# The second pair of layer one in block products of two units, with its weight parts in DRAM and the next layer's x operands made from chunks in DRAM

## The chip, the core and the metric

The program runs on one core of a Trainium2 chip. The metric is the device time of one execution in microseconds (us); of several runs the median is given. A profiled execution gives the trace, and its span runs from the first instruction to the last.

## The reference

Sigmoid attention, then two feed-forward layers on 1792 tokens (4 sequences of 448) of 768 channels, 2048 hidden units each. Everything is float32.

```python
scores = scale * q @ k.T - log(S)          # 4 x 12 heads, S = 448, D = 64
x = (1 / (1 + exp(-scores))) @ v           # heads side by side: 1792 x 768
h = x @ w1_in;  x = relu(h) ** 2 @ w1_out
h = x @ w2_in;  out = (max(h, 0) + alpha * min(h, 0)) @ w2_out
```

The weights come in as 64-bit words, whose halves the kernel joins to float32 itself (`raw` to `words`: two ScalarE scalings, one VectorE join).

## The kernel before

Every float32 product is made of three TensorE products of rounded parts, high x high, high x low and low x high (`HIGH + LOW`), so each operand is first split: ScalarE copies the high part, VectorE or GpSimd subtracts to get the low one.

The feed-forward work is cut into 32 units. A unit is (layer, pair, fp): a pair is two sequences (896 tokens), fp is one of 8 groups of 256 hidden units (two `j` of 128). This gives four stages of eight units, called here 1A and 1B (layer one, first and second pair) and 2A and 2B (layer two). A unit has an inward part (x by w_in) and an outward part (hidden by w_out, added to the output `acc`).

**Inward** (`add_inward`, `product`): the product of 256 hidden units by 896 tokens over 768 channels is done as 2 x 2 blocks with seven block products in place of eight. `X[0..6]` hold the parts of seven x operands (three 128-channel chunks each), `W` those of seven weight operands (`OPERAND` slots). Each of the seven products is nine matmuls of 448 columns into a bank `h`. `x_sum` and `x_high`/`x_low` make the x operands from the pair's `acc`; for the next stage some of them are made ahead by GpSimd (`add_waiting`) through `stage` and kept in DRAM (`kept_x`). `weight_sum`, `weight_high` and `weight_low` make the weight operands of a unit from `words`.

**Outward**, two forms. In stages 1A, 1B and 2A (`add_outward`, `out_product`) a unit's hidden block `G[j]` meets `WO[j]` at once: per j three ways, in layer one with 512 or 384 tokens as moving columns, twelve outputs. In 2B only, `out_block` treats two neighbouring units together: their hidden values are left unsplit in `E[0]` and `E[1]`, sums of blocks are made, and seven block products of 18 matmuls each replace eight. Parts of hidden sums go through a ring of `G` slots, parts of weight sums through a ring of `WO` slots; `collect` and `gather` add the banks to `acc`. Its weight operands come from DRAM: 2A stores `W` (`kept_w`) and 2B loads it (`add_weights_kept`); layer two's words are loaded and joined during 1B (`add_words`) and recalled in 2A (`add_recall`).

The order of all this is set by `Plan`: each step is a job with an engine, an estimated duration, what it reads and writes. `Plan.run` gives each job a due time counted back from TensorE's own fixed order, and fills every engine's queue by due time; SP's queue issues the DMAs in that order, and each engine works its queue in order.

Of the kernel before, what the change touches and what calls it, by code (L numbers as in the profile page):

```python
# [19 lines left out]
class Plan:  # L20
# [4 lines left out]

    HOP = 0.10
    MARGIN = 3.0
# [19 lines left out]
    def run(self):  # L47
# [6 lines left out]
        def length(j):  # L54
            return jobs[j][1] if jobs[j][0] != "SP" else jobs[j][5] / 0.28e6 + 2.0
# [24 lines left out]
        def choose(e):  # L80
# [8 lines left out]
            for j in now:  # L89
                end = t + jobs[j][1]  # L90
                if not any(due[s] < due[j] and begin(s, free[e]) < end and end > due[s] - self.MARGIN for s in soon):
                    return t, j
# [3 lines left out]
        while len(order) < n:  # L96
            t, j, e = min((*c, e) for e in engines if (c := choose(e)))
# [8 lines left out]
            if e == "SP" or size:  # L106
                dma_free = max(dma_free, t + 0.1) + size / 0.28e6
                end = dma_free + 2.0
# [12 lines left out]
def fused_kernel(ctx: ExitStack, tc: tile.TileContext, q, k, v, w1i, w1o, w2i, w2o, alpha, out):  # L121
# [47 lines left out]
    W = wpool.tile([P, 2, 7 * HALF], F32R, name="wi")  # L169
    sums = wpool.tile([P, 4 * HALF], F32, tag="sums", name="sums")  # L170
    both_words = wpool.tile([P, 4 * DM], F32, name="words")
    words = {kind: both_words[:, i * 2 * DM:(i + 1) * 2 * DM].rearrange("p (j m) -> p j m", j=2) for i, kind in enumerate("io")}
    raw = [wpool.tile([P, DM, 2], I32, tag=f"raw{i}", name=f"raw{i}") for i in range(2)]
    late = dpool.tile([P, NC * PAIR], F32, name="late")
    kept = {}
# [3 lines left out]
    def load(at, n, kind, j):  # L179
# [4 lines left out]
        d = raw[at].rearrange("p m t -> p (m t)").bitcast(I64)  # L184
# [5 lines left out]
    def scale(at, word):  # L190

        half = raw[at][:, :, word]
        if word:
            nc.scalar.activation(half.bitcast(F32), half.bitcast(F32), AF.Prelu, scale=2.0 ** -112, alpha=2.0 ** 32)  # L194
        else:
            nc.scalar.activation(half, half.bitcast(U32), AF.Copy, scale=2.0 ** -29 * (1 - 2.0 ** -12), bias=-0.5 + 7.5 * 2.0 ** -12)  # L196

    def joined(at, n, kind, j):

        if UNITS[n][0] == 0:  # L200
            return words[kind][:, j].bitcast(I32)
        return raw[at].rearrange("p m t -> p (m t)")[:, :DM]

    def join(at, n, kind, j):

        nc.vector.scalar_tensor_tensor(out=joined(at, n, kind, j), in0=raw[at][:, :, 1], scalar=3, in1=raw[at][:, :, 0], op0=ALU.logical_shift_left, op1=ALU.bitwise_or)
# [66 lines left out]
    with tc.manual_schedule():  # L273
# [6 lines left out]
        with tc.tile_pool(name="apool", bufs=1) as apool, tc.tile_pool(name="apsum", bufs=1, space=bass.MemoryType.PSUM) as psum:  # L280
# [153 lines left out]
            for d in range(ND):  # L434
# [37 lines left out]
                if item:  # L472
                    join(i % 2, *item)
                    keep(i % 2, *item)
# [38 lines left out]
        def product(k, bank, halves):  # L513

            ps = hb[bank][:, :S]
            for c in range(KH):
                at = OPERAND[k] * HALF + c * P
                for i, (wp, xp) in enumerate(((0, 0), (0, 1), (1, 0))):
                    ends = [0, S // 2, S] if halves and c == 0 and i == 0 else [0, S]
                    for a, e in zip(ends, ends[1:]):  # L520
                        nc.tensor.matmul(ps[:, a:e], W[:, wp, at:at + P], X[k][:, xp, c, a:e], start=(k in OPENING and c == 0 and i == 0 and a == 0), stop=(c == KH - 1 and i == 2), skip_group_check=True)  # L521
# [55 lines left out]
        LAST = NU - NB  # L577

        def blocks(n):

            return (UNITS[n][2] % 2, False) if n >= LAST else (0, True)

# [11 lines left out]

        def cells_of(p, name, c):
            kh, t = PLACE[name]
            return [("acc", p, ((kh * KH + c) * 2 + t) * S // CELL + k) for k in range(S // CELL)]
# [15 lines left out]
        def add_words(n, kind, j):  # L613

            at = at_raw[0] % 2
            at_raw[0] += 1
            high, low = ("raw", at, 1), ("raw", at, 0)
            layer, p, fp = UNITS[n]
            to = [("words", kind, j)] if layer == 0 else [high, low]
            add("SP", 0.05, lambda: load(at, n, kind, j), [], [high, low], size=2 * DM * BYTES)  # L620
            add("ACT", act(DM), lambda: scale(at, 1), [high], [high])
            add("ACT", act(DM), lambda: scale(at, 0), [low], [low])
            add("DVE", dve(DM), lambda: join(at, n, kind, j), [high, low], to, port=True)
            add("SP", 0.05, lambda: keep(at, n, kind, j), to, [("kept", layer, 2 * fp + j, kind)], size=DM * BYTES)

        def add_recall(n, kind, j):
            layer, p, fp = UNITS[n]
            add("SP", 0.05, lambda: recall(n, kind, j), [("kept", layer, 2 * fp + j, kind)], [("words", kind, j)], size=DM * BYTES)
# [3 lines left out]
        def add_weights(n):  # L632

            for what, reads in (("s12", ["s0", "s1"]), ("s34", ["s2", "s3"]), ("a1", [("words", "i", 0)]), ("a2", [("words", "i", 1)])):
# [5 lines left out]
                if UNITS[n][:2] == (1, 0):  # L640
                    a, e = SLOTS[what][0] * HALF, (SLOTS[what][-1] + 1) * HALF
                    to = w_kept[UNITS[n][2]] = w_kept.get(UNITS[n][2]) or dpool.tile([P, 2, 7 * HALF], F32, name=f"kept_w{n}")
                    add("SP", 0.05, lambda a=a, e=e, to=to: nc.sync.dma_start(out=to[:, :, a:e], in_=W[:, :, a:e].bitcast(F32)), [("w", s, i) for s in SLOTS[what] for i in range(2)], [("kept_w", UNITS[n][2], s) for s in SLOTS[what]], size=2 * (e - a) * BYTES)

# [14 lines left out]
        def add_weights_kept(n):  # L659

            for k in OPERAND:
# [377 lines left out]
```

## Time and profile before

| what | value |
|---|---|
| median of 3 runs | 1028.1 us (1028.08 to 1028.81) |
| the profiled execution's own time | 1027.84 us |
| its span | 1026.0 us |
| TensorE busy | 1019.7 us (99%) |
| VectorE, ScalarE, GpSimd busy | 710.3, 635.9, 297.4 us |
| DMA | 209.79 MB, mean 204 GB/s |
| TensorE clock granted | 1.0 throughout |

In the trace attention runs to 158.49 us; the four stages begin at 158.49, 377.73, 596.02 and 816.14 us (the first inward product of each). PE is TensorE, PEld its weight loads, DVE VectorE, ACT ScalarE, POOL GpSimd, SP the queue that issues the DMAs.

### The profile page before, as it was taken

To read this page: it belongs to the slowest core of one execution; us is meant where nothing else is said; L and a number is where in the kernel's file an instruction comes from. 1 tells how busy PE (TensorE), PEld (TensorE's weight loads), DVE (VectorE), ACT (ScalarE), POOL (GpSimd) and SP (SyncE) were. 2 spreads that over 40 slices of the span, in tenths; PEclk is the share of its full clock that TensorE was granted. 3 is DMA by queue.
4 is the path that set the end of the run, shared out by engine and by line. 5 is a ranking of instruction groups with operands and counts; after the bars stand their busy time and mean duration, and the time that the engine had idled before them with its cause. 6 is when DMAs were issued, how large, how long until landed. Compare 5 with 4: busy or idle time off the path is not lost.

```text
span 1026.0 us, 15038 instructions
## 1 busy us (share of the span) xinstructions
PE 1019.7 (99%) x5591; PEld 895.3 (87%) x5591; DVE 710.3 (69%) x951; ACT 635.9 (62%) x995; POOL 297.4 (29%) x258
## 2 busy tenths in 40 slices
PE   9999999999999999999999999999999999999998
PEld 5555558998999999999999999999999999999998
DVE  5555986567776775877666665777766667685857
ACT  4567778866776668666666767555545465535352
POOL 0001233364211142542111231354112207170603
PEclk9999999999999999999999999999999999999999
DMA  7577746566665785566555877688655882727133
GB/s 151 141 190 197 204 133 233 193 211 216 190 229 164 260 321 200 187 225 222 197 188 200 329 288 261 229 292 301 224 207 188 309 265 95 213 67 211 35 104 108
DMA packets 146584, 209.79 MB, mean 204 GB/s; under 512 B 56528, under 2 KB 115408, under 8 KB 144976
## 3 DMA queue, kind: packets, MB, share of 16 engines
q1 hardware_dynamic: 143632, 207.00, 61.3%
q10 hardware_dynamic: 2880, 1.84, 0.6%
q8 instruction: 44, 0.72, 0.3%
q14 instruction: 28, 0.23, 0.1%
HBM read 138.22 MB, written 70.58 MB: 204 GB/s over the span
## 4 chain that ended last, share of the span: by engine, by line
PE 88%; issue 3%; DMA 3%; DVE 3%; POOL 2%; ACT 1%; SPq 0%; POOLq 0%; DVEq 0%; ACTq 0%
PE h L521 35%; PE o L544 27%; PE o L863 6%; PE av L374 5%; PE sc L354 4%; PE h L863 4%; PE h L544 2%; POOL wo L649 1%; PE tp L321 1%; PE av L382 1%; PE scr L364 1%; DMA raw<-in_moe_w_out_dram 1%; PE tp L324 1%; DMA words<-kept21o 1%; DVE acc L785 1%
## 5 line engine op out<-in xcount | busy, mean ns | idle before, releaser
L521 PE MATMUL h<-x,wi 128*128 128x448 f32 (+1 forms) x2072 | 418.1, 360 | 0.1
L521 PEld LDWEIGHTS h<-x,wi 128*128 128x128 f32 x2072 | 380.0, 188 | 29.6 <-issue 0.7
L544 PE MATMUL o<-g,wo 128*128 128x512 f32 (+1 forms) x1056 | 223.3, 366 | 0.1
L544 PEld LDWEIGHTS o<-g,wo 128*128 128x128 f32 x1056 | 192.7, 188 | 23.2 <-DVE acc L785 0.5
L649 POOL TENSOR_TENSOR wo<-words,wo 128x384 fp32r<-128x384 f32 x96 | 99.4, 1066 | 236.5 <-ACT wo L652 235.1
L785 DVE TENSOR_TENSOR acc<-o,acc 128x768 f32<-128x768 f32 (+2 forms) x133 | 128.8, 973 | 24.2 <-PE o L544 23.7
L711 DVE TENSOR_TENSOR c<-h,c 128x448 f32<-128x448 f32 x84 | 52.3, 623 | 127.8 <-PE h L521 127.6
L544 PE MATMUL o<-wo,g 128*128 128x384 f32 x624 | 113.0, 335 | 0.4 <-DVE g L694 0.3
L544 PEld LDWEIGHTS o<-wo,g 128*128 128x128 f32 x624 | 109.1, 188 | 1.4 <-DVE g L694 1.0
L694 DVE TENSOR_TENSOR g<-c,g 128x448 fp32r<-128x448 f32 x96 | 64.3, 675 | 40.2 <-ACT c L682 34.2
L356 ACT ACTIVATE a<-sc,bias 128x896 f32<-128x896 f32 x72 | 69.2, 1005 | 35.6 <-PE av L374 22.6
L652 ACT ACTIVATE wo<-words 128x768 fp32r<-128x768 f32 x48 | 38.3, 840 | 84.2 <-PE o L544 52.9
L268 POOL TENSOR_TENSOR stage<-acc,stage 128x448 fp32r<-128x448 f32 x33 | 42.7, 1294 | 154.6 <-ACT stage L265 154.6
L707 ACT ACTIVATE c<-h 128x448 f32<-128x448 f32 x84 | 45.5, 543 | 55.4 <-PE h L521 55.1
L194 ACT ACTIVATE raw<-raw 128x768 f32<-128x768 f32 x64 | 57.8, 903 | 28.9 <-DMA raw<-in_moe_w_in_dram 20.0
L374 PE MATMUL av<-a,v 128*64 128x448 f32 x288 | 59.4, 548 | 0.0
L847 POOL TENSOR_TENSOR wo<-acc,wo 128x384 fp32r<-128x384 f32 x24 | 29.2, 1239 | 99.1 <-ACT wo L842 99.0
L196 ACT ACTIVATE raw<-raw 128x768 int32<-128x768 uint32 x64 | 57.5, 898 | 0.0
L261 POOL TENSOR_TENSOR acc<-acc 128x448 f32<-128x448 f32 x40 | 55.1, 1382 | 8.3 <-DMA acc<-late 6.3
L244 DVE TENSOR_TENSOR wi<-sums,wi 128x768 fp32r<-128x768 f32 x48 | 50.0, 1046 | 5.2 <-ACT wi L240 5.2
L690 DVE SCALAR_TENSOR_TENSOR c<-c,nal,pos 128x448 f32<-128x448 f32 x48 | 34.8, 726 | 14.9 <-ACT c L689 13.4
L268 POOL TENSOR_TENSOR x<-acc,x 128x448 fp32r<-128x448 f32 x15 | 18.1, 1218 | 88.3 <-ACT x L265 88.3
(140 smaller groups left out, 1393.6 us busy)
## 6 DMA issues: line engine op xcount, KB each, us to landing
raw<-in_moe_w_in_dram SPq DMA_DIRECT2D x32, 768.0 KB, 5.4
raw<-in_moe_w_out_dram SPq DMA_DIRECT2D x32, 768.0 KB, 5.6
wi<-kept_w SPq DMA_DIRECT2D x56, 384.0 KB, 4.2
kept_w<-wi SPq DMA_DIRECT2D x24, 768.0 KB, 5.3
kept_x<-stage SPq DMA_DIRECT2D x33, 448.0 KB, 4.2
x<-kept_x SPq DMA_DIRECT2D x11, 1344.0 KB, 10.3
v<-in_v_dram SPq DMA_DIRECT2D x24, 192.0 KB, 2.9
nat<-in_q_dram SPq DMA_DIRECT2D x22, 192.0 KB, 3.6
```

What stands on the lines that cost most here:

```text
L194: nc.scalar.activation(half.bitcast(F32), half.bitcast(F32), AF.Prelu, scale=2.0 ** -112, alpha=2.0 ** 32)
L196: nc.scalar.activation(half, half.bitcast(U32), AF.Copy, scale=2.0 ** -29 * (1 - 2.0 ** -12), bias=-0.5 + 7.5 * 2.0 ** -12)
L261: eng.tensor_sub(to, x, y)
L268: eng.tensor_sub(lo, x_block(p, X_FROM[i], c), hi)
L356: nc.scalar.activation(sig[u, j], ps[:, :, :S], AF.Sigmoid, bias=bias[:, :1], scale=SCALE)
L374: nc.tensor.matmul(avs[u][h * D:(h + 1) * D, :S], vals[u][:, h, j, :], a[:, h, :], start=(u % 2 == 0 and j == 0), stop=(u % 2 == 1 and j = ...
L521: nc.tensor.matmul(ps[:, a:e], W[:, wp, at:at + P], X[k][:, xp, c, a:e], start=(k in OPENING and c == 0 and i == 0 and a == 0), stop=(c == ...
L544: nc.tensor.matmul(ps, *ops, start=(begin and i == 0), stop=(end and i == len(ways) - 1), skip_group_check=True)
L649: nc.gpsimd.tensor_sub(WO[j][:, 1, at], words["o"][:, j, at], WO[j][:, 0, at])
L694: add("DVE", dve(S), lambda: nc.vector.tensor_sub(gl, e, gh), [*key, h_key], [l_key], port=True)
L785: add("DVE", dve(count), lambda dst=dst, src=src: nc.vector.tensor_add(dst, src, dst), [*src_keys, *cells], cells)
L863: nc.tensor.matmul(ps, left(gi, j), right(wi)[:, j], start=(start and j == 0 and i == 0), stop=(j == 1 and i == 2), skip_group_check=True)
```

## The change

1B takes the form of 2B. Its outward products go through `out_block`, in layer one with weight parts as the stationary operand and hidden parts as the moving one, 448 columns wide. `E[1]` and two weight sums (`TT`) lie in pair 0's `acc[0]` in both layers, so 1A's last unit stores `acc[0]` to DRAM (`hidden`), and 2A's x operands are made in 1B from chunks loaded back into a spare stretch of it (`pieces`): all seven for chunks 0 and 1, three for chunk 2, kept in DRAM. 1A stores its weight parts, 1B loads them. Layer two's words are in the main loaded, scaled and joined in 2A itself, the two inward ones by one transfer (`load_both`). X steps ahead of 2B are on VectorE in place of GpSimd (`X_BY`). The planner's transfer time follows the run length (`moved`), and its rules for SP and GpSimd change.

```diff
-    MARGIN = 3.0
+    MARGIN = 2.5
+    DEPTH = 3.0
 ...
+            if jobs[j][0] == "SP":
+                t = max(t, dma_free - self.DEPTH)
 ...
+                if e == "POOL" and give_way and any(jobs[s][4] and due[s] < min(due[j], end) and max(free["DVE"], ready[s]) < end for s in waiting["DVE"]):
+                    continue
 ...
+    def in_place(n, kind, j):
+        return UNITS[n][0] == 0 or UNITS[n][2] > 0 and (kind == "i" or j == 1)
 ...
+    PIECES = 4 * S + 2 * DM
+    pieces = acc[0][:, PIECES:PIECES + 4 * S].rearrange("p (k t s) -> p k t s", k=2, t=2)
 ...
+        def moved(size, run):
+
+            return size / run * (0.037 + run / 30e3) / 16
 ...
+                if fp == NB - 1 and layer == 0:
+                    c, at = os[0][0], TOKENS[os[0][1]]
+                    add("SP", 0.05, lambda part=part, c=c, at=at: nc.sync.dma_start(out=hidden.rearrange("p (c s) -> p c s", c=NC)[:, c:c + 2, at], in_=part), cells, [("hidden", cell[2]) for cell in cells], size=moved(2 * size * BYTES, 4 * size))
 ...
+            WIDE = MAIN if layer else S
+            RING = {"g": 2 + layer, "wo": 3 + layer}
 ...
-                    add("PE", 6 * PE_OUT[HALF], lambda i=i, left=left: matmuls(banks[at][i][:, :HALF], left, ws, start), gk + wk, [bank_keys[at][i]])
+                    def stationary(ways, j, i=i):
+                        return (gs(ways[0]) if layer else ws(ways[1]))[:, j, i * P:(i + 1) * P]
+
+                    def moving(ways, j):
+                        return (ws(ways[1]) if layer else gs(ways[0]))[:, j]
 ...
+        X_BY = ("POOL", "POOL", "DVE")
 ...
+            elif p:
                 add_weights_kept(n)
 ...
-            if NB <= n < 2 * NB:
-                for kind in "io":
-                    for j in range(2):
-                        add_words(n + NB, kind, j)
+            elif layer == 0:
+                for kind, j in (("i", 0), ("i", 1), ("o", 0), ("o", 1)) if fp == 0 else (("o", 0),):
+                    add_words(n + NB, kind, j)
 ...
-            outward = add_outward(n) if n < LAST else None
+            outward = add_outward(n) if p == 0 else None
 ...
-                    if i < (3 if layer else 4):
+                    chunks = KH if i < (3 if layer or by_pieces else 4) else KH - 1 if by_pieces else 0
```

How the order moves, first on TensorE (PE) after the last inward product of 1B's first unit before, and of its first two units now (`h`, `o`: banks; `g`: hidden parts; `wo`, `ring_sums`: slots of weight parts). Before:

```order
L521 MATMUL h_1790<-x_74,wi 128x448 x8
L544 MATMUL o_1789<-g_1786,wo_1784 128x384 x6
L544 MATMUL o_1793<-g_1786,wo_1784 128x384 x6
L544 MATMUL o_1794<-g_1786,wo_1784 128x384 x3
L544 MATMUL o_1794<-g_1785,wo_1783 128x384 x3
L544 MATMUL h_1792<-g_1786,wo_1784 128x384 x3
L544 MATMUL h_1792<-g_1785,wo_1783 128x384 x3
L544 MATMUL o_1789<-g_1786,wo_1784 128x512 x3
L544 MATMUL o_1789<-g_1785,wo_1783 128x512 x3
```

Now:

```order
L555 MATMUL h_1784<-x_74,wi 128x448 x9
L942 MATMUL o_1785<-g_1777,wo_1775 128x224 x2
L942 MATMUL o_1785<-g_1777,wo_1775 128x448 x11
L942 MATMUL o_1786<-g_1777,wo_1775 128x448 x6
L942 MATMUL h_1782<-g_1778,wo_1776 128x224 x2
L942 MATMUL h_1782<-g_1778,wo_1776 128x448 x5
L942 MATMUL h_1783<-g_1778,wo_1776 128x448 x6
L942 MATMUL h_1784<-g_1778,wo_1776 128x448 x6
L942 MATMUL o_1785<-g_1777,ring_sums 128x224 x2
L942 MATMUL o_1785<-g_1777,ring_sums 128x448 x11
```

Blocks of 18 full matmuls, alternating between the `o` and the `h` banks and between two `g` slots, stand in place of the 512 and 384 wide ones.

Second, VectorE (DVE) beside such outward products, in 1B's fourth unit before and among the block products of its second pair now (`acc_1787` and `acc_1779`: the output; L973 gathers, L921 low parts, `pos` and `c` among them sums of hidden blocks). Before:

```order
L785 TENSOR_TENSOR acc_1787<-o_1789,acc_1787 128x2x384
L244 TENSOR_TENSOR wi<-sums,wi 128x768
L785 TENSOR_TENSOR acc_1787<-o_1794,acc_1787 128x384
L785 TENSOR_TENSOR acc_1787<-h_1792,acc_1787 128x384
L224 TENSOR_TENSOR sums<-words 128x384
L226 TENSOR_TENSOR sums<-sums,words 128x384
L785 TENSOR_TENSOR acc_1787<-o_1793,acc_1787 128x2x512
```

Now:

```order
L973 TENSOR_TENSOR acc_1779<-o_1786,acc_1779 128x448
L973 TENSOR_TENSOR acc_1779<-h_1782,acc_1779 128x448
L973 TENSOR_TENSOR acc_1779<-h_1783,acc_1779 128x448
L973 TENSOR_TENSOR acc_1779<-h_1784,acc_1779 128x448
L921 TENSOR_TENSOR g_1778<-acc_76,g_1778 128x896
L973 TENSOR_TENSOR acc_1779<-o_1785,acc_1779 128x448 x2
L921 TENSOR_TENSOR wo_1775<-words,wo_1775 128x768
L973 TENSOR_TENSOR acc_1779<-o_1786,acc_1779 128x448
L921 TENSOR_TENSOR g_1777<-c,g_1777 128x896
```

The weight work is gone from there; each `g` slot's low part follows three gathers.

Third, VectorE in the middle of stage 2A, the stretch from a unit's last `acc` row on (L206 and L231 join words, L302 and L295 are x steps). Before:

```order
L206 SCALAR_TENSOR_TENSOR raw_81<-raw_81 128x768
L785 TENSOR_TENSOR acc_76<-o_1793,acc_76 128x768
L206 SCALAR_TENSOR_TENSOR raw_80<-raw_80 128x768
L711 TENSOR_TENSOR c<-h_1792,c 128x448
L690 SCALAR_TENSOR_TENSOR c<-c,nal,pos 128x448
L694 TENSOR_TENSOR g_1785<-c,g_1785 128x448
```

Now:

```order
L840 TENSOR_TENSOR acc_76<-o_1785,acc_76 128x768
L231 SCALAR_TENSOR_TENSOR words<-raw 128x768
L302 TENSOR_TENSOR stage<-acc_1779,stage 128x448
L295 TENSOR_TENSOR acc_1779<-acc_1779 128x448
L766 TENSOR_TENSOR c<-h_1784,c 128x448
L745 SCALAR_TENSOR_TENSOR c<-c,nal,pos 128x448
L749 TENSOR_TENSOR g_1777<-c,g_1777 128x448
```

In both a unit's hidden work (from L711, now L766, on) follows. Ahead of it stood joins in some units of 2A only (ten in the stage); now every unit but the first has three of its own, and x steps that were on GpSimd.

## Rows read from the trace of the kernel before

**Rows 1.** The page, part 1: busy us, share of the span, instructions.

```profile
PE 1019.7 (99%) x5591; PEld 895.3 (87%) x5591; DVE 710.3 (69%) x951; ACT 635.9 (62%) x995; POOL 297.4 (29%) x258
```

**Rows 2.** Waits of the weight loads, 158 to 1026 us: total, times, longest (three largest).

```profile
PEld o L544 <- DVE g L694: 1.0, 2, 0.7
PEld h L521 <- issue: 0.7, 1, 0.7
PEld o L544 <- DVE acc L785: 0.5, 1, 0.5
```

**Rows 3.** Chain of waits, one unit of stage 1B: start us, us, what.

```profile
432.30 10.96 PE h L521 x55
443.26 2.10 PE o L544 x12
445.37 1.84 PE h L521 x10
447.20 3.14 PE o L544 x18
450.35 1.04 PE h L544 x6
451.39 8.20 PE o L544 x36
```

**Rows 4.** Chain of waits, one pair of units of stage 2B.

```profile
867.73 25.57 PE h L521 x128
...
897.49 3.12 PE h L863 x18
```

**Rows 5.** VectorE's groups by line, 867.73 to 919.33: busy, mean ns | idle before.

```profile
L830 DVE TENSOR_TENSOR acc<-words 128x768 f32<-128x768 f32 x3 | 4.3, 1437 | 0.0
...
L711 DVE TENSOR_TENSOR c<-h,c 128x448 f32<-128x448 f32 x3 | 1.9, 625 | 2.1 <-PE h L521 2.1
...
L830 DVE TENSOR_TENSOR c<-c 128x768 f32<-128x768 f32 x1 | 1.0, 958 | 0.0
```

**Rows 6.** Groups by line and form, whole span.

```profile
L261 POOL TENSOR_TENSOR acc<-acc 128x448 f32<-128x448 f32 x40 | 55.1, 1382 | 8.3 <-DMA acc<-late 6.3
...
L206 DVE SCALAR_TENSOR_TENSOR words<-raw 128x768 int32<-128x768 int32 x32 | 35.5, 1114 | 4.8 <-ACT raw L196 4.8
...
L847 POOL TENSOR_TENSOR wo<-acc,wo 128x384 fp32r<-128x384 f32 x24 | 29.2, 1239 | 99.1 <-ACT wo L842 99.0
...
L268 DVE TENSOR_TENSOR x<-acc,x 128x448 fp32r<-128x448 f32 x36 | 25.9, 750 | 3.8 <-ACT x L265 3.8
...
L842 ACT ACTIVATE g<-c 128x768 fp32r<-128x768 f32 x8 | 6.7, 839 | 3.6 <-DVE c L830 3.6
```

**Rows 7.** Timeline of VectorE in stage 2B: start us, us.

```profile
908.36 1.77 DVE L844 TENSOR_TENSOR g<-acc,g 128x768 fp32r<-128x768 f32 x1
...
912.85 0.94 DVE L844 TENSOR_TENSOR g<-pos,g 128x768 fp32r<-128x768 f32 x1
```

**Rows 8.** Timeline of GpSimd at the same place.

```profile
906.35 2.97 POOL L847 TENSOR_TENSOR ring_sums<-words,ring_sums 128x384 fp32r<-128x384 f32 x2 [0.75 <-ACT ring_sums L842]
```

**Rows 9.** Windows, a pair of 2B: PE, PEld, DVE, ACT, POOL, clock, DMA, GB/s.

```profile
867.73:919.33 51.60, 51.60 (x281) 49.77 (x280) 37.18 (x54) 25.66 (x41) 19.78 (x17) 1.00 0.48 139
```

**Rows 10.** Windows, stages 1B and 2A.

```profile
376.73:595.02 218.29, 218.29 (x1098) 199.62 (x1097) 148.03 (x196) 145.97 (x238) 66.92 (x60) 1.00 0.63 220
595.02:816.14 221.12, 220.73 (x1199) 212.86 (x1198) 155.74 (x220) 124.88 (x211) 64.02 (x57) 1.00 0.70 253
```

**Rows 11.** Windows, around the boundary of 1B and 2A.

```profile
577.00:602.00 25.00, 25.00 (x128) 22.83 (x127) 19.00 (x25) 17.63 (x31) 10.78 (x10) 1.00 1.02 413
```

**Rows 12.** Windows, sum of four units of 2A, 650.83 to 761.34.

```profile
sum 110.51, PE 110.12 PEld 105.95 DVE 85.15 ACT 62.58 POOL 37.34; mean PE 27.53 PEld 26.49 DVE 21.29 ACT 15.65 POOL 9.33
```

**Rows 13.** Windows of the joins (L206) alone: DVE, clock, DMA, GB/s.

```profile
595.02:816.14 221.12, 9.61 (x10) 1.00 0.70 253
650.83:761.34 110.51, 6.77 (x7) 1.00 0.72 254
```

More of the change, by code (lines that the diff above doesn't have):

```diff
@@ L639, in add_weights, with add_weights_store @@
                 add("DVE", dve(cols), lambda what=what: weight_low(what), [*reads, *(("w", s, 0) for s in SLOTS[what])], [("w", s, 1) for s in SLOTS[what]], port=True)
[L640 to L643, printed above, removed]
+                add_weights_store(n, SLOTS[what])
+        def add_weights_store(n, slots):
+            layer, p, fp = UNITS[n]
+            if (layer, fp) not in w_kept:
+                w_kept[layer, fp] = dpool.tile([P, 7, 2, HALF], F32, name=f"kept_w{n}")
+            a, e, to = slots[0], slots[-1] + 1, w_kept[layer, fp]
+            add("SP", 0.05, lambda: nc.sync.dma_start(out=to[:, a:e], in_=W[:, a:e].bitcast(F32)), [("w", s, i) for s in slots for i in range(2)], [("kept_w", layer, fp, s) for s in slots], size=moved(2 * (e - a) * HALF * BYTES, 8 * (e - a) * HALF))
         def add_out_weights(n):
@@ L740, in add_store @@
             cells, emit = held.pop()
-            add("SP", 0.1, emit, [*cells, *after], [], size=DM * BYTES)
+            add("SP", 0.1, emit, [*cells, *after], [], size=moved(DM * BYTES, 4 * DM))
         def add_outward(n):
@@ L892, in put @@
                     part, cells = place(row, e)
-                    add("SP", 0.1, lambda: store(p * PAIR + at, part[first:first + size], slice(e * HALF, (e + 1) * HALF), (nc.sync, nc.scalar)), cells, [], size=size * HALF * 4)
+                    add("SP", 0.1, lambda: store(p * PAIR + at, part[first:first + size], slice(e * HALF, (e + 1) * HALF), (nc.sync, nc.scalar)), cells, [], size=moved(size * HALF * 4, 4 * HALF))
             def collect(at, row, e, first=True, last=False):
                 for i in range(3):
-                    gather(banks[at][i][:, :HALF], bank_keys[at][i], place(row + i, e), first)
+                    gather(banks[at][i], bank_keys[at][i], place(row + i, e), first)
                     if last:
@@ L954, in fused_kernel, with add_pieces @@
+        def add_pieces(c):
+            kept_cells = [("hidden", ((kh * KH + c) * 2 + t) * S // CELL + k) for kh in range(2) for t in range(2) for k in range(S // CELL)]
+            add("SP", 0.05, lambda: nc.sync.dma_start(out=pieces, in_=hidden.rearrange("p (k c t s) -> p k c t s", k=2, c=KH, t=2)[:, :, c]), kept_cells, old_cells(PIECES, 4 * S), size=moved(4 * S * BYTES, 8 * S))
         for n in range(NU):
             layer, p, fp = UNITS[n]
+            other, phase = 1 - p, n // NB
+            by_pieces = phase == 1
+            if fp == 0 and phase in (1, 3):
+                ring_at.update(g=0, wo=0)
+                if phase == 3:
+                    add_ring("raw", [("raw", i, t) for i in range(2) for t in range(2)] + [("both", i) for i in range(2)], ("g", 2), ("wo", 2))
+                add_ring("sums", [f"s{i}" for i in range(4)], ("wo", phase // 2 + 2))
```

252 lines of the change are left out of this document (152 added, 100 removed).

## The prediction

> **What bounds the kernel now.** First the page's busy shares: TensorE is busy 1019.7 of 1026.0 us [rows 1], so a shorter time has to come from TensorE's work or from its few waits. Then its weight loads' waits over the four stages, where a stop of TensorE shows: 2.2 us in the three largest groups, of which 1.0 is on VectorE's `g` (L694), twice, both in stage 2A [rows 2]. So from 158 us on the time is the sum of the matmuls, and I read their prices off the chain of waits, where each piece's length is what TensorE spends on it end to end (the mean ns of a group overlaps the next matmul). A unit of stage 1B is 10.96 us for 54 inward matmuls of 448 columns (one of them in two halves, hence x55), 1.84 for nine more, and 2.10, 3.14, 1.04 and 8.20 for the outward ones: 27.28 us [rows 3]. In stage 2B two units' inward products take 25.57 us for 126 full matmuls (x128 with the halves), and a block product of 18 matmuls of 384 columns 3.12 us [rows 4]. Dividing: 448 columns cost 0.203 us both times, 384 cost 0.174, 512 cost 0.228. The first figure is the same in 1B, at 220 GB/s of DMA traffic, as in this pair of 2B, at 139 [rows 9, 10], so I don't let matmuls get slower with more transfers.
>
> **Part 1, the outward products of stage 1B (removes TensorE time).** Before, a unit's outward part is 2.10 + 3.14 + 1.04 + 8.20 = 14.48 us [rows 3], eight units 115.8 us. After, each pair of units has 7 block products of 18 matmuls of 448 columns (the order on PE shows it); 7 x 18 x 0.203 = 25.6 us, four pairs 102.3 us. The halved first matmul costs nothing more: x55 and x10 have the same 0.203 per full matmul. **Gain 13.5 us**, all of it on the path.
>
> **Part 2, what stands beside those products.** A pair in 1B lasts 25.6 + 25.6 = 51.2 us. VectorE's work in it, counted in the order: 21 gathers and 6 totals that read PSUM, at 0.625 (same form as the `c<-h` row), 16.9 us; 11 sums and low parts of 896 columns, at 0.96 x 896/768 = 1.12 (the undisturbed `c<-c` row of 768), 12.3; 7 of 768 columns at 0.96, 6.7; 2 joins at 1.11, 2.2: 38 us [rows 5, 6]. That hides under 51.2, if each piece comes in time. The tightest place is the ring: only two `g` slots, so the slot of product i must be refilled while product i+1 runs (18 x 0.203 = 3.65 us). ScalarE's copy and VectorE's low part are about 0.98 + 1.12 = 2.1 us (0.84, rows 6, and 0.96 scaled), and three gathers of 0.625 can stand ahead: 4.0 us in the worst order. The order does put the finished product's three gathers ahead of the low part, but two of them read rows of it that are done while the third still runs, so one gather stands in the way, beside ScalarE's copy: 2.1 to 2.7 of 3.65. I take 0; bounds 0 and 0.35 x 5 refills x 4 pairs = 7 us. GpSimd is weighed here too. The rows show that a VectorE instruction with two SBUF inputs stands still while GpSimd runs: the same 768-column subtraction takes 0.94 us alone and 1.77 when it comes up at 908.36 [rows 7], a us ahead of the end of a GpSimd stretch [rows 8]. The Trainium skill's page "SBUF — State Buffer", section "Who interferes with whom", says the same as a rule: such an instruction and a GpSimd instruction that reads SBUF exclude each other, and the second one blocks fully. Taken at its worst, that rule speaks against this change, because 1B now has more of both; that is rival D. What rows give: in a pair of 2B, VectorE was busy 37.18 us and GpSimd 19.78 [rows 9], and its instructions over their undisturbed price add up to some 4 us (three `acc<-words` at 1.437 for 0.96 are 1.4 of it, rows 5), a fifth of GpSimd's time. GpSimd in a pair of 1B: 8 low parts at 1.24 and 10 x steps at 1.38, 23.7 us [rows 6]; a fifth is 4.7, so VectorE needs some 43 of 51.2 us. Cost 0.
>
> **Part 3, weight parts from DRAM.** Gone from 1B: 4 sums, 4 high and 4 low parts per unit and the recall of 4 words; in their place 7 loads of 384 KB, and in 1A 4 stores per unit. Counted on SP in the order: 67 stores of parts for 32, 112 loads of them for 56, 11 recalls for 64, 34 words kept for 64, 32 word loads of block products for 16; with `hidden`, its chunks and the x tiles about +31 MB on 209.8. DMA moved 220 GB/s in 1B and 253 in 2A [rows 10], and 413 over 25 us at the boundary of the two [rows 11]. The new mean, about 240 MB in 1015 us, is 237. Cover: a slot's load starts when unit n's product of that slot ends and is needed a unit (25 us) later. Cost 0.
>
> **Part 4, the joins move from 1B into stage 2A, and the x steps of 2A from GpSimd to VectorE.** This is where I charge something. 2A had VectorE at 155.74 of 221.12 us with 10 joins, 9.61 us [rows 10, 13]. After: 21 joins at 1.11 (+13.8 us) and 21 x steps at 0.75 (+15.8) [rows 6]: 185 us, 84%. In the middle units it is denser: the four units from 650.83 on have 85.15 us [rows 12] with 7 joins, 6.77 us [rows 13]: 19.6 a unit without them, plus three joins and 3.5 x steps 25.5 of 27.4 us, 93%; about one us comes off because GpSimd's x steps no longer stop VectorE. At under 80% it already made TensorE wait twice, 1.0 us in all [rows 2]. Bounds: 0 (minus the 1.0 if even those go), and one wait of 0.66 in each of 8 units, 5.3 us. I take a wait in every second unit, 2.6 us, **1.6 us more than before**: nearer the lower end, since no unit is over 100%.
>
> **Part 5, the boundaries.** At 1B's end 7 x tiles come from DRAM (3 x 1.38 + 4 x 0.92 MB), one double word load (1.57) and the recall of unit 16's words (0.79): 10.2 MB, 25 us at 413 GB/s [rows 11]. They start as unit 15's products release the tiles, from 9 us ahead of the last block products on, and those cover 25.6 us. The recall is the late one: its buffer is free only when `t1`'s parts are made, some 12 us into the block products; the x tiles ahead of it are through at about 14, it lands at about 18, and four sums and the first parts (about 4 us) end at 22 of 25.6. Queued behind it on VectorE are the gathers of products 6 and 7. Price 0, bounds 0 and +3 if it lands 7 us later. At 1A's end 2.75 MB of `hidden` are added beside the x tiles; the tiles overwritten are `acc` columns first written 12.8 us later. Price 0, upper 2.
>
> The planner's other edits (MARGIN, DEPTH, GpSimd giving way, transfer times by run length) change orders on VectorE, GpSimd and SP, not TensorE's; cover is TensorE's own work, and if that were gone it is the waits of parts 2 and 4, counted there.
>
> **Sum.** -13.5 + 1.6 = -11.9 us. The profiled execution took 1027.84 us, 1.84 of them outside the span; 1027.84 - 11.9 = 1015.9. The median of the runs, 1028.1, is 0.26 above it: **1016 us**.
>
> **Rivals.**
> A, the forecast: 1012.5 to 1018.5. Chance 0.68. Its lower end is the gain of part 1 with 2 us of the old waits gone.
> B, VectorE becomes the bound of 2A: in order, at 93%, a join that waits for a late word load holds totals and low parts behind it, and TensorE stops in every unit, 0.66 to 1.5 us x 7: 1018.5 to 1024. For it: both old waits in 2A are on VectorE [rows 2]. Against: GpSimd stops it less. 0.13.
> C, a boundary runs late: the recall lands behind the x tiles, 3 to 5 us once, 1019 to 1021. For: 413 GB/s is all the trace ever shows. Against: 25.6 us of cover. 0.08.
> D, slower: in stage 1B GpSimd stops VectorE in full. 38 + 23.7 = 61.7 us against 51.2 for a pair, four pairs +42, less 13.5: about 1056. It decides from the point where VectorE's pair is longer by 3.4 us than TensorE's, that is when 0.7 of GpSimd's time stops VectorE, for which the trace of 2B has a fifth. With the ring's 7 us and 5 of B added, 0.57 is enough. 0.06.
> E, it doesn't do what it says: the outward gain is eaten by waits of the same size at each block product (0.48 us x 28), no net change, 1026 to 1030. 0.04.
> What is left, 0.01, lies below 1012.5.
>
> **Numbers.** About 0.2% (2 us) is what a measurement of this kernel tells from no change. Faster by more: A, B and C, what lies below A, and E's lower end (0.01), 0.91; within: the rest of E, 0.03; slower: D, 0.06. The range 1012.5 to 1021.5 holds A, C and half of B, 0.82.
>
> **What would show it.** Right: in 1B the chain has pieces of 25.6 us inward and seven of 3.65 us per pair, the stage lasts 204.6 us for 218.3, and TensorE's busy time falls by 13.5. Part 4 right: VectorE at 80 to 85% over 2A and TensorE's waits there 2 to 3 us. Wrong: weight loads of block products that wait for `g` or `ring_sums` (D, E); a gap at the first inward product of 2A with a DMA as releaser (C); more than 5 us of waits on VectorE in 2A (B); a 448-column block matmul off 0.203.

## The result and the profile after

The changed kernel takes **1018.28 us** (median of 4 runs, 1016.98 to 1018.99) against 1028.18 for the kernel before on the same chip: ratio 0.9901, 95% interval 0.9884 to 0.9918. The forecast was 1016.0, with a range of 1012.5 to 1021.5. The time is inside the range, 2.3 us above the forecast, and the terms did not all come out as forecast. The profiled execution took 1018.92 us, 1017.1 of them in the span.

First the page's busy shares, which answer to [rows 1]:

```profile
PE 1008.2 (99%) x5539; PEld 886.6 (87%) x5539; DVE 730.2 (72%) x968; ACT 636.6 (63%) x976; POOL 281.0 (28%) x240
```

TensorE lost 11.5 us of busy time (forecast 13.5). VectorE is busy 20 us longer, GpSimd 16 us shorter. Transfers rose to 237.6 MB (forecast: about 240).

The windows of the four stages 1A, 1B, 2A and 2B, with the columns of [rows 9] (us, then PE, PEld, DVE, ACT and POOL busy, clock, DMA share, GB/s), show where the time went:

```profile
159.01:379.94 220.93, 219.90 (x1099) 199.41 (x1099) 151.53 (x196) 152.37 (x243) 69.36 (x59) 1.00 0.79 292
379.94:588.13 208.19, 206.18 (x1047) 190.33 (x1046) 153.25 (x185) 134.11 (x208) 77.12 (x62) 1.00 0.85 307
588.13:807.32 219.19, 219.19 (x1195) 212.05 (x1194) 178.52 (x257) 141.89 (x230) 38.86 (x35) 1.00 0.68 249
807.32:1017.10 209.78, 206.37 (x1112) 198.72 (x1111) 142.77 (x203) 102.96 (x170) 76.72 (x64) 1.00 0.46 143
```

The stages before began at 158.49, 377.73, 596.02 and 816.14 us and the span ended at 1026.0, so against them:

| stretch | before | after | change | forecast change |
|---|---|---|---|---|
| attention, to the first inward product of 1A | 158.49 | 159.01 | +0.52 | 0 |
| 1A | 219.24 | 220.93 | +1.69 | 0 |
| 1B | 218.29 | 208.19 | -10.10 | -13.5 |
| 2A | 220.12 | 219.19 | -0.93 | +1.6 |
| 2B | 209.86 | 209.78 | -0.08 | 0 |

The chain of waits over a pair of 1B (start us, us, what) has the pieces that part 1 forecast: seven block products of 448 columns, six of them at 3.67 us and the seventh with a 0.12 us stop, and 25.6 inward.

```profile
405.52 3.67 PE o L942 x19
...
423.85 3.67 PE h L942 x19
427.52 3.79 PE o L942 x19
431.30 25.59 PE h L555 x128
```

The waits of the weight loads over the four stages (total, times, longest), which answer to [rows 2]:

```profile
PEld o L578 <- DVE acc L840: 2.4, 4, 1.2
PEld h L555 <- DVE c L766: 2.0, 1, 2.0
PEld h L555 <- issue: 0.7, 1, 0.7
PEld o L578 <- DVE g L749: 0.7, 1, 0.7
PEld h L942 <- DVE g L921: 0.7, 1, 0.7
...
```

The first and fourth groups lie in 1A, the second and fifth in 1B; the third is at the first product of 1A. None, of the smaller ones either, lies in 2A, where I had charged 2.6 us. With the two smaller ones of 1B (0.4 and 0.2) the waits there sum to 3.3 us, all in its third pair of units.

**The wait in 1A.** The chain of waits ahead of 1A's longest stop:

```profile
304.49 10.74 DMA raw<-in_moe_w_in_dram
...
316.03 0.90 ACT raw L218
...
317.83 1.02 DVE acc L840 x2
318.84 0.88 DVE words L231
...
322.05 3.02 PE o L578 x12
```

A double load of words (1536 KB, new in this kernel) takes 10.74 us to land. ScalarE's scaling and VectorE's join (L231) come late for it, and the gathers of TensorE's finished outward products (`acc`, L840) stand behind the joins on VectorE.

**The wait in 1B.** VectorE, GpSimd and SP ahead of the 2.0 us in the third pair of units (timeline, other rows left out):

```profile
473.26 0.57 SPq L1048 DMA_DIRECT2D acc<-hidden  x1
...
474.58 1.56 SPq L890 DMA_DIRECT2D words<-kept5o  x2
...
484.66 0.96 DVE L905 TENSOR_TENSOR acc<-words 128x768 f32<-128x768 f32 x1 [1.32 <-POOL stage L302]
...
488.79 1.79 DVE L905 TENSOR_TENSOR acc<-words,acc 128x768 f32<-128x768 f32 x1
489.85 3.57 POOL L295 TENSOR_TENSOR acc<-acc 128x448 f32<-128x448 f32 x2
490.51 1.90 DVE L231 SCALAR_TENSOR_TENSOR raw<-raw 128x768 int32<-128x768 int32 x1
492.33 1.90 DVE L921 TENSOR_TENSOR wo<-acc,wo 128x768 fp32r<-128x768 f32 x1
...
494.16 0.95 DVE L231 SCALAR_TENSOR_TENSOR raw<-raw 128x768 int32<-128x768 int32 x1
495.03 1.67 DVE L766 TENSOR_TENSOR c<-h,c 128x448 f32<-128x448 f32 x3
...
496.23 1.08 PE L555 MATMUL h<-x,wi 128*128 128x448 f32 x4 [1.62 <-DVE c L766]
```

Two candidates meet here: words that are issued just behind a chunk load of `hidden`, and three VectorE instructions that take 1.79 to 1.90 us beside GpSimd's x steps where their like take 0.95 or 0.96 alone (L905 at 484.66, L231 at 494.16). The first of these, L905 at 484.66, had itself waited 1.32 us for an x step of GpSimd. The experiments had to part them.

### The profile page after: what moved, and what is told of

Read it like the earlier page. It is cut to its first block, busy times and chain, and to the rows that moved or that the text cites. A ratio compares the mean times of both kernels' runs of the same rounds, so it can differ in the third digit from the quotient of the medians.

```text
span 1017.1 us, 15048 instructions
## 1 busy us (share of the span) xinstructions
PE 1008.2 (99%) x5539; PEld 886.6 (87%) x5539; DVE 730.2 (72%) x968; ACT 636.6 (63%) x976; POOL 281.0 (28%) x240
## 4 chain that ended last, share of the span: by engine, by line
PE 90%; DVE 4%; DMA 2%; issue 2%; POOL 1%; ACT 1%; SPq 0%; DVEq 0%; POOLq 0%; ACTq 0%
PE h L555 38%; PE o L578 20%; PE o L942 11%; PE h L942 7%; PE av L408 5%; PE sc L388 4%; PE h L578 1%; DMA raw<-in_moe_w_in_dram 1%; PE scr L398 1%; PE tp L355 1%; PE av L416 1%; DMA words<-kept5o 1%; PE tp L358 1%; DVE flat L361 1%; PE busy L432 0%
## 5 line engine op out<-in xcount | busy, mean ns | idle before, releaser
L700 POOL TENSOR_TENSOR wo<-words,wo 128x384 fp32r<-128x384 f32 x64 | 69.3, 1107 | 242.9 <-ACT wo L703 238.8
L578 PE MATMUL o<-g,wo 128*128 128x512 f32 (+1 forms) x528 | 112.9, 367 | 1.0 <-DVE acc L840 0.8
L578 PEld LDWEIGHTS o<-g,wo 128*128 128x128 f32 x528 | 96.0, 188 | 14.2 <-DVE acc L840 2.4
L840 DVE TENSOR_TENSOR acc<-o,acc 128x768 f32<-128x768 f32 (+2 forms) x91 | 85.6, 950 | 12.9 <-PE o L578 12.7
L766 DVE TENSOR_TENSOR c<-h,c 128x448 f32<-128x448 f32 x72 | 44.6, 622 | 69.2 <-PE h L555 66.9
L749 DVE TENSOR_TENSOR g<-c,g 128x448 fp32r<-128x448 f32 x64 | 43.4, 681 | 31.6 <-ACT c L737 21.5
L302 POOL TENSOR_TENSOR stage<-acc,stage 128x448 fp32r<-128x448 f32 x29 | 35.9, 1237 | 99.2 <-ACT stage L299 99.2
L231 DVE SCALAR_TENSOR_TENSOR words<-raw 128x768 int32<-128x768 int32 x53 | 52.8, 1005 | 9.7 <-ACT raw L218 8.9
L973 DVE TENSOR_TENSOR acc<-o,acc 128x384 f32<-128x384 f32 (+1 forms) x84 | 46.1, 580 | 14.7 <-PE o L942 14.4
L295 POOL TENSOR_TENSOR acc<-acc 128x448 f32<-128x448 f32 x28 | 40.6, 1451 | 27.9 <-DMA acc<-late 16.2
L408 PEld LDWEIGHTS av<-a,v 128*64 128x64 f32 x288 | 18.5, 136 | 28.7 <-issue 26.8
```

The lines of the kernel that those rows point to most:

```text
L231: nc.vector.scalar_tensor_tensor(out=to, in0=raw_words(at, 1, both), scalar=3, in1=raw_words(at, 0, both), op0=ALU.logical_shift_left, op1 ...
L408: nc.tensor.matmul(avs[u][h * D:(h + 1) * D, :S], vals[u][:, h, j, :], a[:, h, :], start=(u % 2 == 0 and j == 0), stop=(u % 2 == 1 and j = ...
L578: nc.tensor.matmul(ps, *ops, start=(begin and i == 0), stop=(end and i == len(ways) - 1), skip_group_check=True)
L700: nc.gpsimd.tensor_sub(WO[j][:, 1, at], words["o"][:, j, at], WO[j][:, 0, at])
L766: add("DVE", dve(S), lambda: nc.vector.tensor_add(to, hb[b][:, :S], to), [("h", b), *key], key)
L840: add("DVE", dve(count), lambda dst=dst, src=src: nc.vector.tensor_add(dst, src, dst), [*src_keys, *cells], cells)
```

## The experiments

Stage lengths of all runs, each from first inward matmul to first inward matmul of the next stage on TensorE's timeline; the medians are of all timed executions of the run.

| kernel | median us | ratio to before, 95% interval | 1A | 1B | 2A |
|---|---|---|---|---|---|
| before | 1028.2 | 1 | 219.2 | 218.3 | 220.1 |
| changed | 1018.3 | 0.9884 to 0.9918 | 220.9 | 208.2 | 219.2 |
| single_loads | 1020.1 | 0.9904 to 0.9934 | 219.5 | 209.2 | 220.5 |
| no_chunks | 1020.0 | 0.9901 to 0.9934 | 220.1 | 207.8 | 221.1 |
| x_by_vector_1b | 1043.0 | 1.013 to 1.016 | 221.2 | 212.4 | 238.1 |
| x_by_gpsimd_2a | 1021.0 | 0.9910 to 0.9942 | 221.9 | 209.0 | 221.1 |
| no_gpsimd_x_1b | 1015.7 | 0.9862 to 0.9892 | 220.1 | 205.0 | 220.0 |
| old_rules | 1028.0 | 0.9989 to 1.0007 | 219.8 | 218.7 | 219.2 |
| no_depth_rule | 1033.0 | 1.0032 to 1.0065 | 219.8 | 216.4 | 223.8 |
| no_give_way | 1023.4 | 0.9939 to 0.9972 | 220.0 | 213.3 | 219.2 |
| latency_4 | 1031.9 | 1.0022 to 1.0043 | 218.4 | 208.3 | 233.0 |
| latency_4_single | 1032.5 | 1.0023 to 1.0048 | 218.4 | 208.4 | 235.4 |
| latency_4_in_1a | 1020.4 | 0.9897 to 0.9930 | 218.4 | 208.9 | 221.0 |
| before_new_rules | 1030.4 | 1.0012 to 1.0031 | 218.6 | 218.3 | 221.9 |

In six of these kernels (changed, no_chunks, x_by_vector_1b, x_by_gpsimd_2a, no_gpsimd_x_1b, no_give_way) every engine has the same instructions in the same order through 1A, and 1A took 220.0 to 221.9 us. So a stage length that differs by under 2 us in a single execution is no evidence by itself.

### 1A: double loads

```diff
-                            add_words(n, kind, j, kind == "i")
+                            add_words(n, kind, j, kind == "i" and layer == 1)
```

> The changed kernel, but in stage 1A a unit's two inward words are loaded by two transfers of 768 KB, as before, in place of one of 1536 KB. Theory 1: 1A lost time (220.9 us from its first inward product to that of 1B, 219.2 before) because the double load takes 8.9 us in the median (10.7 at 304.5 us), and the join that waits for it stands ahead of the gathers in VectorE's queue; with single loads (5.4 us before) 1A goes back to 219.3 us or less and the waits of TensorE on the acc additions there (2.4 us) fall under 1 us. Rival 1: the stores of weight parts fill the DMA engines and any word load is late; then 1A stays at 220.5 us or more.

1A took 219.5 us, between the two theories and just under the six like executions, and its waits on the gathers went from 2.4 us to 0.7; the whole became no faster, since 1B (209.2) and 2A (220.5) waited more in this order. One execution does not settle it.

The planner's figure for a transfer tells more. It counts 2.0 us beside the time by bytes and run length (`moved`): for a double load that comes to 5.05 + 2.0 = 7.1 us, for a single one of 768 KB to 3.4 + 2.0 = 5.4, with nothing queued ahead (the 5.5 of the expectation below is that figure). The inward word loads of 1A took these times from issue to landing, first in the kernel before (single), then in the changed one (double), then in single_loads:

```profile
DMA to landing us min/median/max: 4.8/5.4/7.6
DMA to landing us min/median/max: 7.8/9.5/11.7
DMA to landing us min/median/max: 5.2/7.0/10.4
```

Before, with 230 GB/s in 1A, single loads landed in the time of that figure. Now, with 292 and 301 GB/s there, both kinds land later than counted: double ones by 2.4 us and single ones by 1.6. So it is not the double load alone; that the new stores of weight parts delay any word load (rival 1) has these times for it, and no run leaves the stores out. What a run can change is when the loads are planned. With 4.0 in place of 2.0:

```diff
-            return jobs[j][1] if jobs[j][0] != "SP" else jobs[j][5] + 2.0
+            return jobs[j][1] if jobs[j][0] != "SP" else jobs[j][5] + 4.0
...
-                end = dma_free + 2.0
+                end = dma_free + 4.0
```

> The planner counts 4.0 us instead of 2.0 for a transfer beside its bytes, so loads are planned earlier; nothing else is edited. Theory A (both losses, 1A's 1.7 us and part of 1B's 3.6 us, come from loads that take 8 to 11 us where the planner counts about 5.5): 1A comes to 219.2 to 220.2 us, 1B to 205.5 to 207.5, the whole 1014.5 to 1017 us. Theory B (the loads collide however early they are planned, or the earlier loads crowd out other work on the queue): stages within 0.8 us of 220.9, 208.2, 219.2, 209.8, or 2A and its boundary lose what the others win; the whole 1017 to 1020 us.

> As the run before (4.0 us of the planner's for a transfer), and layer one's inward words of weights are loaded one block at a time instead of two. Theory A (double loads are slower to land, which cost 1A 1.4 us, and loads are planned too short, which costs 1B): 1A 219.0 to 219.8 us, 1B 205.5 to 207.5, the whole 1014 to 1016.5 us. Theory B (the two are the same fault seen twice, or single loads crowd the queue in 1B as they seemed to before, where 1B took 209.2 and 2A 220.5): 1A 219.5, 1B 208 to 209.5, 2A over 220, the whole 1018 to 1021 us.

1A is 218.4 us in both, without a wait of TensorE, but the boundary from 1B to 2A breaks, and the whole is 13.6 and 14.2 us slower than the changed kernel. The chain of waits of the first of these, at that boundary:

```profile
584.84 1.75 POOL acc L295
...
590.21 0.14 POOL x L302
...
591.33 2.70 POOL wo L700 x2
...
594.05 0.32 SPq L245
...
594.78 7.75 DMA x<-kept_x
...
602.66 1.46 PE h L555 x3
```

The last x steps of GpSimd are late, and the x load (L1107) stands on SP behind a recall of words (L245) that waits for GpSimd's low parts. That is the place of rival C, though with the x load behind the recall and not the recall behind the x loads, at 14 and 16 us more in 2A instead of its 3 to 5. The next kernel keeps 4.0 to 1A:

```diff
+            plan.extra = LATENCY[phase]
...
+        LATENCY = (4.0, 2.0, 2.0, 2.0)
```

> 4.0 us instead of 2.0 for a transfer beside its bytes, in the planner's figures for stage 1A alone, so that the loads of 1A are planned earlier and the boundary from 1B to 2A, at which the run with 4.0 everywhere stopped for 11 us, is planned as in the changed kernel. Theory A (1A's 217.7 us in that run came from the earlier loads, and its 11 us from late x operands at that boundary alone): 1A 217.5 to 218.5 us, 1B 207 to 209.5, no stop over 2 us at 1B's end, the whole 1014 to 1016.5 us. Theory B (1A varies by 2 us between executions anyway, 219.3 to 221.9 for the same instructions, and 217.7 was chance): 1A 219 to 222, the whole 1017 to 1020.

The 217.7 us of this expectation was counted from 158.9 us on; from the first inward product, as in the table, that run's 1A is 218.4. The window of 1A in the new run:

```profile
158.79:377.18 218.39, 218.39 (x1098) 199.70 (x1099) 150.53 (x196) 152.65 (x243) 69.18 (x59) 1.00 0.79 295
```

For 1A theory A holds: 218.39 us, all of it TensorE busy, the third execution without a wait there. The traffic is that of the changed kernel (295 GB/s for 292), so it is not the traffic as such that delays 1A: the loads are planned too late for the time they take beside it. Three executions at 218.4 us stand against six at 220.0 to 221.9. For the whole theory B came out, 1020.4 us: 2A began with a wait for first parts (L274) and lost 1.8 us against the changed kernel, 2B 1.4 and 1B 0.7. It beats the kernel before, not the changed one.

### 1B: late words or GpSimd

```diff
                         if what == "load":
-                            add_pieces(c)
+                            pass
```

This leaves out the chunk loads of 1B, so layer two's x operands are made from other data.

> The changed kernel without the three loads of 1792 KB that bring chunks of hidden back in stage 1B; the x steps still run, on whatever lies in the pieces. Left out: the right x operands of stage 2A. Theory 2: 1B lost 3 us at 476 to 496 us because the second chunk load is issued 1.3 us ahead of the words of the next block products, which then take 8.1 us to land, so that VectorE makes the weight sums late and the totals of the next inward products stand behind them; without the chunk loads 1B falls from 208.2 us to 205 to 206. Rival 2: GpSimd's x steps, which stop VectorE (1.79 and 1.90 us for 0.95), make the wait; then 1B stays at 207.5 us or more, since GpSimd's work is the same.

The wait at 496 us is gone, but 1B is still 207.8 us. TensorE waits elsewhere, in the first pair of 1B at 413.56 and 421.57 us:

```profile
PEld o L942 <- DVE ring_sums L921: 1.5, 1, 1.5
PEld o L942 <- DVE wo L921: 0.6, 1, 0.6
...
```

So the late words decide where 1B stops, not how long. The other candidate, GpSimd's x steps:

```diff
-        X_BY = ("POOL", "POOL", "DVE")
+        X_BY = ("POOL", None, "DVE")
```

with the steps left out where the engine is None.

> GpSimd's x sums and x differences of stage 1B are left out (their stores, the chunk loads and ScalarE's roundings stay), so layer two's x operands are not the right ones. Theory A (the 3.6 us that 1B loses against its 204.6 us of products come from VectorE being held up by GpSimd's x steps, with or without late weight parts): 1B falls from 208.2 to between 204.7 and 206 us, the waits on VectorE's totals and ring weights sum to under 1 us, and the whole is 1014.5 to 1016.5 us. Theory B (the loss comes from weight parts that land late behind the chunk loads, and GpSimd has no part in it): 1B stays at 207 to 209 us, with a wait of 1 to 2 us near 496 us or one like it.

Its window of 1B:

```profile
378.25:583.20 204.95, 204.95 (x1046) 190.59 (x1045) 142.70 (x184) 135.20 (x209) 37.39 (x35) 1.00 0.85 313
```

204.95 us, all of it TensorE busy, with the chunk loads in place and 313 GB/s. GpSimd is busy 39.7 us less than in the changed kernel (77.12 to 37.39), and VectorE, with as much work of its own, 10.55 us less (153.25 to 142.70): 0.27 of GpSimd's time had been added to VectorE's. Theory A holds: in the seven other runs that keep these steps on GpSimd and the planner's new rules, the changed kernel among them, 1B takes 207.8 to 209.2 us. The Trainium skill's page "SBUF — State Buffer", section "Who interferes with whom", has such pairs of instructions exclude each other; the stretched rows agree, and the cost here is about a quarter of GpSimd's time. Why it is no more was not measured. The edit also lets the planner put VectorE's queue in another order, and it removes waits for the x steps themselves, such as the 1.32 us at 484.66, together with the stretching; this run does not part them.

Moving the same steps to VectorE is no way out:

```diff
-        X_BY = ("POOL", "POOL", "DVE")
+        X_BY = ("POOL", "DVE", "DVE")
```

> The changed kernel with the x steps of stage 1B on VectorE in place of GpSimd (29 instructions). Theory 2 (late words): 1B keeps its 208 us within 1 us or gets longer, since the words still land late and VectorE has 20 us more work. Rival 2 (the shared port): 1B falls to 206 us or less, because VectorE is no longer stopped.

1B itself ran up to its last block product without a wait, in 205.15 us, with VectorE as busy as in the changed kernel (154.07 us for 153.25) and GpSimd at 38.08:

```profile
380.05:585.20 205.15, 205.15 (x1045) 190.39 (x1043) 154.07 (x206) 132.98 (x204) 38.08 (x32) 1.00 0.80 287
```

So it is not VectorE's amount of work that stops 1B, and rival 2 holds there. But the x steps fell behind on VectorE and 2A's first products stopped for 7.2 us on first parts and for 14.3 on an x tile:

```profile
592.42 7.92 PE L555 MATMUL h<-x,wi 128*128 128x224 f32 x28 [7.22 <-DVE wi L273]
614.67 7.17 PE L555 MATMUL h<-x,wi 128*128 128x448 f32 x27 [14.32 <-DMA x<-kept_x]
```

### 2A: x steps back on GpSimd

```diff
-        X_BY = ("POOL", "POOL", "DVE")
+        X_BY = ("POOL", "POOL", "POOL")
```

> The changed kernel with the x steps of stage 2A on GpSimd, as before, in place of VectorE (21 steps). Theory 3: stage 2A lost nothing after the change (219.19 us, no wait of TensorE, at 178.5 us of VectorE) because these steps on VectorE stop nothing, while on GpSimd they hold VectorE's instructions; then 2A gets waits again, 220.0 us or more, and GpSimd's time there rises from 39 to some 64 us. Rival 3: the engine of the steps doesn't matter, the planner's rules removed the waits; then 2A stays at 219.2 to 219.5 us.

2A took 221.1 us, with three waits:

```profile
PEld h L555 <- ACT wi L269: 1.1, 1, 1.1
PEld h L555 <- DVE wi L273: 0.7, 1, 0.7
PEld h L555 <- ACT c L762: 0.4, 1, 0.4
```

Eight units of 2A at 27.4 us without a wait (each of the middle ones in latency_4_in_1a) are 219.2 us, which is what 2A takes in the changed kernel. Here 1.9 is lost. But no_chunks, with these steps on VectorE, lost as much in 2A (221.1 us, with waits of up to 0.6 us at 596 to 735 us), and the other kernels that kept them there and passed the boundary took 219.2 to 221.0. So this run does not tell whether taking GpSimd's steps out is what freed 2A.

### The planner's rules

The prediction gave the planner's edits no price. First all three taken back:

```diff
-    MARGIN = 2.5
-    DEPTH = 3.0
+    MARGIN = 3.0
...
-            if jobs[j][0] == "SP":
-                t = max(t, dma_free - self.DEPTH)
...
-                if e == "POOL" and give_way and any(jobs[s][4] and due[s] < min(due[j], end) and max(free["DVE"], ready[s]) < end for s in waiting["DVE"]):
-                    continue
```

> The changed kernel with the planner's rules as they were before the change: margin 3.0 us, no limit on how far transfers queue up, and GpSimd does not give way to VectorE's due work. TensorE's sequence of products is the same. Theory A (the new rules are part of why stage 2A lost no time in the changed kernel, where I had forecast 1.6 us more of waits): 2A goes back from 219.2 to 220.0 us or more, and 1B, where GpSimd now also takes x steps, goes from 208.2 to 209.5 or more; the whole 1020 to 1024 us. Theory B (the new rules are neutral, 2A's waits went because six joins in it became loads): every stage within 0.8 us of the changed kernel's 220.9, 208.2, 219.2, 209.8, the whole 1017 to 1019.5 us.

1028.0 us: **the whole gain is gone**, all of it in 1B (218.7 us), while 2A stays at 219.2. Both theories were half right, and the three rules are not what freed 2A. The start of 1B in its timeline:

```profile
385.88 2.33 SPq L839 DMA_DIRECT2D hidden<-acc  x3
...
388.81 0.33 SPq L710 DMA_DIRECT2D wi<-kept_w  x1
...
...
397.40 3.01 PE L551 MATMUL h<-x,wi 128*128 128x224 f32 x8 [4.80 <-DMA wi<-kept_w]
```

and its windows there:

```profile
385.00:397.40 12.40, 6.14 (x30) 5.08 (x29) 5.44 (x7) 6.47 (x10) 0.00 (x0) 1.00 1.04 406
397.40:401.00 3.60, 3.60 (x11) 3.29 (x12) 3.53 (x5) 1.12 (x2) 0.00 (x0) 0.53 1.04 410
401.00:405.00 4.00, 4.00 (x21) 3.64 (x20) 1.56 (x2) 1.72 (x4) 0.00 (x0) 1.00 1.03 412
```

The weight part for the second unit is issued behind the stores of `hidden` while all DMA engines are taken (share 1.04, 406 GB/s), lands 8.5 us later, and TensorE stops for 4.80 us. After it the clock granted is 0.53 for 3.6 us, in which 11 matmuls start where 4.0 us at full clock have 21. A second stop, again with a low clock behind it (0.51 from 581.70 to 585.20), stands near the end of 1B, on VectorE's low part of `g`:

```profile
580.77 5.07 PE L938 MATMUL h<-g,wo 128*128 128x448 f32 x16 [2.91 <-DVE g L917]
```

Against 1B without waits, 204.95 us, 13.8 us are lost: 9.2 in these two stops and one of 1.46 us at 386.89, and about 3 by the clock, an estimate from the matmuls counted above. Then each of two rules alone (MARGIN alone was not run):

```diff
             if jobs[j][0] == "SP":
-                t = max(t, dma_free - self.DEPTH)
+                pass
```

> Of the planner's three new rules one is taken back: transfers may again be queued however many are under way. The run with all three taken back took 1028.0 us, with 1B at 218.7, its weights from DRAM landing 8.5 us after issue at the start of 1B (4.8 us of stop, then half clock). Theory A (this rule carries most of the 10 us): the whole 1022 to 1028 us, with a stop of over 3 us on a transfer within the first 25 us of 1B. Theory B (GpSimd's giving way carries them): the whole under 1020 us, 1B under 210.

```diff
-        def choose(e, give_way=True):
+        def choose(e, give_way=False):
```

> Of the planner's three new rules only this one is taken back: GpSimd again starts an elementwise step although VectorE has one due sooner. Theory A (the limit on queued transfers carries the 10 us): the whole 1017 to 1020 us, 1B 207.5 to 210. Theory B (GpSimd holding up VectorE carries them): 1022 us or more, with waits on VectorE in 1B of over 6 us in sum.

Without the limit on queued transfers the time is 1033.0 us, 14.7 more than the changed kernel; 1B (216.4 us) has the same stop on `wi<-kept_w`, 5.70 us at 399.42, after one of 2.18, and 2A (223.8) stops for 2.9 us on its first parts and x tiles. Without GpSimd giving way it is 1023.4, 5.1 more; 1B is 213.3 us, with five stops of 5.0 us together, four of them on VectorE, the longest 3.03 on `g` (L921) at 575.73 (clock 0.54 for the 3.5 us after it). So each of the two rules has a price of its own, and it is the one that its theory names: a late transfer for the first, though 1033.0 lies above that theory's 1028, and VectorE held up for the second, though the waits on VectorE there, 4.5 us, stay under its 6. The two prices don't add: their sum is 19.8, all three rules together 9.7.

Last, the same rules on the kernel before:

> The kernel before, whole, with the change's three planner rules alone (margin 2.5, the limit on queued transfers, GpSimd giving way). With it four corners stand: kernel before with old rules 1028.3 us, changed kernel with old rules 1028.0, changed kernel with new rules 1018.3, and this one. Theory A (the rules are needed because of what the change adds, 1B's x steps on GpSimd and its loads; on the kernel before there is little for them to save, since TensorE waits there for under 5 us in all from 1A to 2B): 1024 to 1029 us, 1B within 1.5 us of 218.3. Theory B (the rules are the gain, and the seven block products bring nothing of their own): 1016 to 1021 us.

1030.4 us, 2.4 slower than the kernel before, with 1B at 218.3. It is a little beyond theory A's 1029 and clearly not theory B. With that the four corners stand:

| | old rules | new rules |
|---|---|---|
| before | 1028.1 | 1030.4 |
| changed | 1028.0 | 1018.3 |

Neither part of the change gains anything without the other. (The planner's new transfer time `moved` goes with the change and not with the three rules, in both rows.)

## Why the prediction was right or wrong

**Part 1 was right.** A block product is 3.67 us for the forecast 3.65, a pair 51.3 us for 51.2, and 1B without waits 204.95 us for 204.6.

**Part 2 named the right mechanism and sized it too small.** "Cost 0" for the ring and GpSimd became 3.2 us (208.19 to 204.95). The step that failed is the sum over a pair: 38 + 4.7 of 51.2 us on VectorE, which as a mean was on the safe side (153.25 / 4 = 38.3 us busy, stretched time and all) and says nothing of a moment at which three stretched instructions stand ahead of a pair's totals. Of the signs of being wrong, a block product's weight load that waits for `g` came once, 0.7 us. GpSimd's share that stops VectorE, a fifth in the prediction, is 0.27; the full stop of rival D did not come. Late words choose the place only.

**Part 3's "cost 0" failed in 1A.** 25 us of cover were counted for the parts, and they were in time; the words of 1A, whose double loads land 2.4 us later there than the planner counts, were not looked at. Price: 220.9 us where 1A without waits is 218.4, against 219.2 before.

**Part 4 had the wrong sign.** VectorE's load was counted somewhat too high, 178.52 of 219.19 us for 185 (81% for 84%), and 22.4 to 23.8 of 27.4 us in the middle units for 25.5: a join took 0.95 us for 1.11 and an x step 0.61 to 0.65 for 0.75. Even so it rose by 23.8 us (154.74 to 178.52), and yet TensorE never waited in 2A: -0.9 us for the forecast +1.6. The step that failed is the one from a busy share to waits: the old waits at under 80% were taken to grow with the share. Why the old ones went stays open: it is not the three planner's rules (219.2 us without them), and whether it is GpSimd's x steps the runs do not tell.

**Part 5 held** in the changed kernel: 1B's end has no stop. How little there was to spare is shown by the kernels that stopped there for 11 to 22 us once x steps or the queue's order changed: at such a place rival C's 3 to 5 us is far too small a price. How likely it was, other kernels do not tell.

**The planner's edits**, set aside in one sentence ("change orders ..., not TensorE's"), are what 9.7 us hang on. The forecast came out because it took for granted that every cover would be served in time, and it is these rules that see to that. That rival E, no net change, is what the rest of the change does with the old rules (1028.0) was not seen, though by a few long stops and not by 28 equal waits.

**The sum.** Against the forecast for the profiled execution, 1015.9: attention +0.5, 1A +1.7, 1B +3.4, 2A -2.5, 2B -0.1, together +3.0, which gives its 1018.9 us. The miss in 2A hid nearly half of the other two; that the whole came within 2.3 us is luck to that extent.

## What to carry to other kernels

Where an engine's work is replaced by loads, price the issue order as a part of its own: ask for each new load what stands ahead of it on its queue, and how long its size takes to land by the trace against what the scheduler counts. A busy share that fits does not show that each piece comes in time, and one that looks full (81% here) need not cost a wait. Test an edit of a scheduler and an edit of the work in all four combinations before giving either the gain.

## What the runs showed of the hardware

A transfer of 1536 KB took 8.9 us (median of 13 in the changed kernel) and 9.0 in latency_4. One of 768 KB in 1A took 5.4 us at the median in the kernel before, beside 230 GB/s, and 7.0 in single_loads, beside 301. The Trainium skill's page "DMA: Bandwidth & Descriptors", section "Anatomy of one DMA — SWDGE (gpsimd) path", fits 2.0 us plus bytes over 436 GB/s, an estimate of 5.6 for 1536 KB; that fit is for transfers issued by GpSimd. These were issued on SP, beside others, and the measurement decides.

After stops of 3.03 and 4.80 us TensorE's granted clock read 0.54 and 0.53 over the next 3.5 and 3.6 us, nearly all at the lower of its two levels, and about 1.5 us were lost by that each time (11 matmuls in 3.6 us, which at 21 in 4.0 take 2.1; the 16 behind the first stop in 4.96 us, for 3.51 us at 528.52 in the same run). After the changed kernel's 1.62 us stop at 496 us it stayed at 1.00.
